# Row maxima of the first 20 steps taken over pairs of key blocks: a + relu(b - a)

## The chip, the core and the metric

The kernel runs on one core of one Trainium2 chip. The metric is the device time of one execution in microseconds (us), lower is better. TensorE is written PE (PEld is its weight load), VectorE is DVE, ScalarE is ACT, GpSimd is POOL, and SP issues the transfers.

## What is computed

One transformer block on 2048 rows of 448: layer norm, attention with 16 heads of 28 that share one key and one value head, a residual, layer norm, a SwiGLU feed-forward with 1792 hidden columns, and a residual.

```python
def _A_ref(x, wq, wk, wv, wo):
    q = (x @ wq).reshape(B, S, H, Dh).transpose(0, 2, 1, 3)
    k, v = x @ wk, x @ wv
    p = softmax(einsum("bhqd,bkd->bhqk", q, k) * Dh ** -0.5)
    o = einsum("bhqk,bkd->bhqd", p, v)
    return o.transpose(0, 2, 1, 3).reshape(B, S, H * Dh) @ wo
def _B_ref(x, w1, w3, w2):
    return (silu(x @ w1) * (x @ w3)) @ w2
h = x + _A_ref(layernorm(x), ...)
out = h + _B_ref(layernorm(h), ...)
```

## The kernel before

The 2048 rows are four tiles `t` of 512. Queries are worked on in 16 items `i = 4 t + g`, one for each tile and each group `g` of four heads; the four heads of a group lie in four lanes of 32 partitions, so four matmuls with 32 rows of weights run side by side in the array. `KH` holds the keys (high part) of all 2048 rows, copied into all four lanes, `KL` the low part, `QR[t]` the queries, `QS[i]` one item's queries, split into a high and a low part.

The softmax needs the maximum of each row of scores before the exponential. An item has 16 steps `(n, kt)`, 128 queries against 512 keys. In a step, `Unit.mm` writes four 128x512 score blocks, one a head, into four PSUM banks, and `Unit.red` reduces each with one DVE `tensor_reduce` to one column of `MX[i]`. A function `quad` does the four units of one step. After 16 steps `max_done` takes the maximum over the four columns and `max_out` writes it, by transfers, into row 28 of `QS[i]`; row 28 of each lane of `KH` holds ones, so that the later score matmul has the maximum already subtracted. In the main loop of 256 steps `Head.mm` makes those scores (three matmuls a head), ACT takes the exponential, `pv` multiplies by the values, and beside them the loop does the units that are `AHEAD = 20` steps further on. So the first 20 steps of units lie ahead of the loop. They are the list `first` of 20 quads, taken out one by one by `quads()`, between the matmuls of the start-up stage: `tr(t)` transposes the normed rows, `kv(t)` makes keys and values of tile `t` in 11 matmuls, `q(t, g)` makes queries in 11 matmuls. `kv` and `q` call `quads` after their sixth matmul (`between`).

All engines run in program order, the order of the Python calls. PSUM has seven banks for all this, handed out by `bank()` in the order in which `done()` gave them back. In `kv(t)`, ACT writes the keys into `KH[0:64]`, then SP issues three transfers one after the other: the copy to `KH[64:128]`, the ones into row 28 of each lane (which must wait for the copy, since two of its rows lie there), and the copy of `KL`.

Of the kernel before, what the change touches and what calls it, by code (L numbers as in the profile page):

```python
# [8 lines left out]
F32 = mybir.dt.float32  # L9
F32R = mybir.dt.float32r  # L10
AF = mybir.ActivationFunctionType
ALU = mybir.AluOpType
# [4 lines left out]
P = 128  # L17
# [5 lines left out]
T = 512  # L23
NT = S // T
NQ = T // P
NG = H // 4
NC = S // P
NF = F // P
NI = NT * NG
EPS = 1e-5  # L30
SCALE = DH ** -0.5
AHEAD = 20
ORDER = "3a u2 w 0a 2a u1 3b 1a 0b 2b 3c 1b 0c 2c u3 v u0 1c".split()
# [4 lines left out]
def block_kernel(  # L38
# [13 lines left out]
    ve, se, ge, pe, sy = nc.vector, nc.scalar, nc.gpsimd, nc.tensor, nc.sync  # L52
# [4 lines left out]
    def f(ap):  # L57
        return ap.bitcast(F32)
# [6 lines left out]
    wk_pool = ctx.enter_context(tc.tile_pool(name="work", bufs=2))  # L65
# [9 lines left out]
    KH = keep.tile([P, S], F32R, name="KH", tag="kh")  # L75
# [37 lines left out]
    def bank(name="pb"):  # L113
        k = free.pop(0)
        ps = ps_w.tile([P, T], F32, name=name, tag=f"bank{k}") if k < 7 else ps_o.tile([P, T], F32, name=name, tag="po")
        used[id(ps)] = ps, k
        return ps

    def done(ps):
        free.append(used.pop(id(ps))[1])  # L120
# [20 lines left out]
    def load_w(dst, w):  # L141
        sy.dma_start(dst[:, 0:3], w[0:384].rearrange("(c p) m -> p c m", p=P))
        sy.dma_start(dst[0:64, 3], w[384:448])
        sy.dma_start(dst[64:128, 3], w[384:448])
# [11 lines left out]
    def ln_stats(t, n):  # L156
        if n == 0:
            LN[t] = (ln_pool.tile([P, NQ, 6], F32, name="st"),
                     ln_pool.tile([P, NQ, 2], F32, name="mv"),
                     ln_pool.tile([P, NQ], F32, name="rs"), {}, ln_pool.tile([P, NQ], F32, name="nb"))  # L160
        st, mv, _, _, _ = LN[t]
        ve.bn_stats(st[:, n], X[t][:, n])  # L162
        ve.bn_aggr(mv[:, n], st[:, n])

    def ln_rstd(t, n0=0, n1=NQ):
        _, mv, rs, _, nb = LN[t]
        ve.tensor_scalar(rs[:, n0:n1], mv[:, n0:n1, 1], EPS, None, op0=ALU.add)
        ge.tensor_tensor(rs[:, n0:n1], rs[:, n0:n1], pexp[:, n0:n1], op=ALU.pow)
# [44 lines left out]
    QS, MX, PT, PO, WH, WS = {}, {}, {}, {}, {}, {}  # L213
# [12 lines left out]
    def lane(j):  # L226
        return slice(32 * j, 32 * j + 32)
# [17 lines left out]
            ve.tensor_reduce(MX[self.i][:, c, self.kt : self.kt + 1], self.ps, axis=AX.X, op=ALU.max)  # L245
            done(self.ps)

    def quad(i, n, kt):
        us = [Unit(i, n, kt, j) for j in range(4)]
        for u in us:  # L250
            u.mm()
        for u in us:
            u.red()

    def max_done(i):

# [11 lines left out]
    class Head:  # L268
# [14 lines left out]
        def exp(self):  # L283
            i, c, (p, jj) = self.i, self.c, divmod(self.j, 2)
            if (i, c, p) not in PT:
                PT[i, c, p] = p_pool.tile([P, 2, T], F32R, name="pt")
            se.activation(f(PT[i, c, p][:, jj]), self.ps, AF.Exp, bias=0.0, scale=SCALE)  # L287
            done(self.ps)
# [78 lines left out]
    with tc.tile_pool(name="start", bufs=1) as sp:  # L367
        wq_r = wo_r = OT[:, :, :D]
        WQ = [w.rearrange("p c (h r) -> p c h r", h=H) for w in OS]
        wkv_r = sp.tile([P, 4, 96], F32, name="wkv_r")  # L370
        WKV = [sp.tile([P, 4, 96], F32R, name=f"WKV{k}") for k in range(2)]
        ones = sp.tile([4, T], F32, name="ones")
        ve.memset(wkv_r, 0.0)
        ve.memset(ones, 1.0)
        ve.memset(VA, 1.0)
        for k in range(2):
            ve.memset(f(NEG[k]), 0.0)
        for k in range(2):
            ve.memset(f(WQ[k][:, :, :, DH:]), 0.0)
        for m0, w in ((0, wk), (64, wv)):  # L380
            load_w(wkv_r[:, :, m0 : m0 + DH], w)
        sy.dma_start(X[1], xv[1])
        load_w(wq_r, wq)
        for t in range(2, NT):
            sy.dma_start(X[t], xv[t])

        def split_wkv():
            ve.tensor_copy(wkv_r[:, :, 32 : 32 + DH], wkv_r[:, :, :DH])
            se.activation(WKV[0], wkv_r, AF.Copy)
            ge.tensor_tensor(WKV[1], wkv_r, f(WKV[0]), op=ALU.subtract)  # L390

        def split_wq():
            wq4 = wq_r.rearrange("p c (h r) -> p c h r", h=H)
            for c in range(4):
                se.activation(WQ[0][:, c, :, :DH], wq4[:, c], AF.Copy)
                eng = ge if c < 2 else ve
                eng.tensor_tensor(WQ[1][:, c, :, :DH], wq4[:, c], f(WQ[0][:, c, :, :DH]), op=ALU.subtract)

        def load_wo():
            ge.memset(wo_r, 0.0)  # L400
            wov = wo.rearrange("(g j r) e -> j r g e", j=4, r=DH)
            for j in range(4):
                sy.dma_start(wo_r[32 * j : 32 * j + DH], wov[j])

        def split_wo(g):
            ve.tensor_copy(WO[0][:, g], wo_r[:, g])
            ge.tensor_tensor(WO[1][:, g], wo_r[:, g], f(WO[0][:, g]), op=ALU.subtract)

        def stats(t, *ns):
            for n in ns:  # L410
                ln_stats(t, n)
            if NQ - 1 in ns:
                ln_rstd(t)

        def norm(t):
            for n in range(NQ):
                ln_norm(t, n)

        def tr(t, *cs):
            for c in cs or range(4):  # L420
                ln_tr(t, c)

        def kv(t, between=None):
            cols = slice(t * T, (t + 1) * T)
            ps = bank()
            mm_D(ps[:96], WKV, XT[t], slice(0, 96), slice(0, T), between)
            se.activation(KH[0:64, cols], ps[0:64], AF.Copy)
            ve.tensor_tensor(KL[0:64, cols], ps[0:64], f(KH[0:64, cols]), op=ALU.subtract)
            vt = sp.tile([P, T], F32, name="vt", bufs=2)
            se.activation(vt[64:96], ps[64:96], AF.Copy)  # L430
            sy.dma_start(f(KH[64:128, cols]), f(KH[0:64, cols]))
            sy.dma_start(f(KH[28::32, cols]), ones)
            sy.dma_start(f(KL[64:128, cols]), f(KL[0:64, cols]))
            done(ps)
            return vt

        def va(t, vt):
            ps = bank()
            for n in range(NQ):
                pe.transpose(ps[:, 32 * n : 32 * n + 32], vt[64:96, n * P : (n + 1) * P], ident[64:96, 64:96])  # L440
            ve.tensor_copy(VA[:, NQ * t : NQ * t + NQ, :DH],
                           ps[:, :P].rearrange("p (n r) -> p n r", n=NQ)[:, :, :DH])
            done(ps)

        def q(t, g, between=None):
            ps = bank()
            mm_D(ps, [w[:, :, 4 * g : 4 * g + 4].rearrange("p c h r -> p c (h r)") for w in WQ],
                 XT[t], slice(0, P), slice(0, T), between)
            if t == g == 0:
                build_qs(0, ps)  # L450
            else:
                se.activation(QR[t][:, g], ps, AF.Copy)
            done(ps)

        first = [(quad, 0, n, kt) for kt in range(4) for n in range(NQ)]
        first += [(max_done, 0), (max_out, 0)]
        first += [(quad, 1, *divmod(c, 4)) for c in range(AHEAD - NC)]

        def quads(n=1):
            while n > 0 and first:  # L460
                fn, *args = first.pop(0)
                fn(*args)
                n -= fn is quad

        for n in range(NQ):
            ln_stats(0, n)
            ln_rstd(0, n, n + 1)
            if n > 0:
                ln_norm(0, n - 1)
        ln_norm(0, NQ - 1)  # L470
        split_wkv()
        tr(0, 0, 1)
        stats(1, 0)
        tr(0, 2)
        stats(1, 1)
        tr(0, 3)
        stats(1, 2, 3)
        split_wq()
        v0 = kv(0)
        norm(1)  # L480
        q(0, 0)
        tr(1)
        stats(2, 0, 1, 2, 3)
        va(0, v0)
        q(0, 1)
        v1 = kv(1)
        norm(2)
        stats(3, 0, 1, 2, 3)
        q(0, 2)
        q(0, 3)  # L490
        build_qs(1)
        tr(2)
        va(1, v1)
        quads()
        v2 = kv(2, quads)
        norm(3)
        q(1, 0, quads)
        quads()
        q(1, 1, quads)
        va(2, v2)  # L500
        quads()
        q(1, 2, quads)
        build_qs(2)
        q(1, 3, quads)
        tr(3)
        v3 = kv(3, quads)
        load_wo()
        for t in (2, 3):
            for g in range(NG):
                if g % 2 == 0:  # L510
                    quads()
                if (t, g) == (2, 1):
                    va(3, v3)
                q(t, g, quads)
        quads(64)
# [16 lines left out]
    for i in range(NI - 1):  # L532
        e = NC * (i + 1)
# [3 lines left out]
    for t in range(NT - 1):  # L537
        e = NC * NG * (t + 1)
# [33 lines left out]
    for s in range(LAST):  # L572
        i, c = divmod(s, NC)
# [156 lines left out]
```

## Time and profile before

| what | us |
|---|---|
| median of 3 runs (lowest, highest) | 1247.76 (1244.99, 1248.25) |
| the profiled execution, its time | 1245.28 |
| the same, span of the trace | 1243.5 |
| PE, DVE, ACT, POOL busy in the span | 1214.8, 892.4, 658.0, 336.5 |
| the 80 reductions of the 20 quads, DVE busy | 48.5 |
| the start-up stage with the quads | 40 to 99.94 |
| the main loop's first matmul | 99.94 |

Times in the trace count from the start of the span. A row of the timeline has its start, its length, engine, line, operation and tiles, how many instructions it stands for, and in brackets the idle time ahead of it and what ended that. Busy PE time is modelled for pipelined matmuls, so PE's pace is read from the starts of consecutive rows.

### The profile page before, as it was taken

What the parts mean: (1) busy time and instruction counts of PE and PEld (TensorE: products, weight loads), DVE (VectorE), ACT (ScalarE), POOL (GpSimd) and SP (SyncE); (2) the same over time, 40 slices, a digit from 0 to 9 for tenths busy, and PEclk for the clock granted to TensorE, in tenths of its full rate; (3) what the DMA queues carried; (4) which work ended last, traced back from release to release, by engine and by line L of the source; (5) the groups of instructions that cost most, each with busy time, mean ns of one, the idle gap of its engine ahead of it and who ended that gap; (6) DMA issues with size and microseconds to landing.
All of it is one profiled execution on the core that took longest, in us unless ns stands there. A gap on an engine that the chain in (4) does not pass through costs nothing. (4 is left out here: it accounts for less than half of the span.)

```text
span 1243.5 us, 25301 instructions
## 1 busy us (share of the span) xinstructions
PE 1214.8 (98%) x10492; PEld 725.0 (58%) x10492; DVE 892.4 (72%) x1474; ACT 658.0 (53%) x1251; POOL 336.5 (27%) x270
## 2 busy tenths in 40 slices
PE   5999999999999999999999999999999999999998
PEld 4665444444544444444444443488888888888876
DVE  7999999999798998898998894144445445444333
ACT  3226888887698886688886688721111111121111
POOL 3201011100112110111110110454555555555552
PEclk8999999999999999999999999999999999999999
DMA  4010001000001000000000010023000000000000
GB/s 160 18 36 2 11 24 45 11 11 2 10 9 38 11 11 2 10 27 20 11 11 1 11 37 11 22 68 105 8 1 30 1 1 30 1 1 30 1 1 30
DMA packets 32411, 27.03 MB, mean 22 GB/s; under 512 B 10840, under 2 KB 28952, under 8 KB 32296
## 3 DMA queue, kind: packets, MB, share of 16 engines
q1 hardware_dynamic: 32296, 25.41, 7.0%
q8 instruction: 82, 1.34, 0.5%
q14 instruction: 33, 0.27, 0.1%
HBM read 20.25 MB, written 3.80 MB: 19 GB/s over the span
## 5 line engine op out<-in xcount | busy, mean ns | idle before, releaser
L245 DVE TENSOR_REDUCE mx<-pa 128x1 f32<-128x512 f32 x1024 | 633.7, 680 | 18.3 <-PE pa L240 6.8
L287 ACT ACTIVATE pt<-pb 128x512 f32<-128x512 f32 x1024 | 530.8, 604 | 144.5 <-PE pb L278 127.4
L278 PE MATMUL pb<-qs,KH 32*128 32x512 f32 x2048 | 368.3, 451 | 3.2 <-ACT pt L287 0.3
L240 PE MATMUL pa<-KH,qs 32*128 32x512 f32 x1024 | 362.2, 469 | 5.8 <-DVE mx L245 2.6
L295 PE MATMUL po<-pt,VA 128*32 128x256 f32 (+1 forms) x3936 | 326.7, 400 | 0.5 <-ACT OT L299 0.5
L278 PE MATMUL pb<-qs,KL 32*128 32x512 f32 x1024 | 274.9, 420 | 0.0
L278 PEld LDWEIGHTS pb<-qs,KH 32*128 32x128 f32 x2048 | 166.7, 182 | 140.4 <-ACT pt L287 89.8
L240 PEld LDWEIGHTS pa<-KH,qs 32*128 32x128 f32 x1024 | 147.3, 181 | 112.8 <-DVE mx L245 99.9
L134 PE MATMUL pa<-xh,qs 128*128 128x512 f32 x784 | 206.2, 396 | 0.0
L134 PEld LDWEIGHTS pa<-xh,qs 128*128 128x128 f32 x784 | 146.7, 188 | 34.5 <-issue 1.2
L622 ACT ACTIVATE rb<-pa 128x512 f32<-128x512 f32 x56 | 30.5, 596 | 253.1 <-PE pa L614 253.1
L295 PEld LDWEIGHTS po<-pt,VA 128*32 128x32 f32 x3936 | 79.8, 108 | 135.5 <-issue 126.8
L639 PE MATMUL pb<-w2s,pt 128*128 128x448 f32 x672 | 144.5, 370 | 0.8 <-POOL w2s L350 0.8
L639 PEld LDWEIGHTS pb<-w2s,pt 128*128 128x128 f32 x672 | 124.0, 188 | 21.0 <-issue 10.2
L278 PEld LDWEIGHTS pb<-qs,KL 32*128 32x128 f32 x1024 | 116.2, 183 | 0.8
L342 POOL TENSOR_TENSOR qs<-QR,qs 128x1024 fp32r<-128x1024 f32 x32 | 88.0, 2766 | 98.7 <-DVE qs L341 98.7
L631 DVE TENSOR_TENSOR pt<-rb,pt 128x512 fp32r<-128x512 f32 x56 | 82.4, 1471 | 39.2 <-ACT pt L630 39.2
L341 DVE CAST qs<-QR 128x1024 fp32r<-128x1024 f32 x32 | 21.0, 688 | 120.5 <-PE pa L614 96.7
L134 PE MATMUL pa<-xl,qs 128*128 128x512 f32 x336 | 96.2, 394 | 0.0
L630 ACT ACTIVATE pt<-rb 128x512 fp32r<-128x512 f32 x56 | 35.5, 633 | 81.5 <-DVE rb L627 81.5
L221 POOL TENSOR_TENSOR qs<-QR,qs 128x512 fp32r<-128x512 f32 x15 | 19.3, 1283 | 206.2 <-ACT qs L220 190.2
L134 PEld LDWEIGHTS pa<-xl,qs 128*128 128x128 f32 x336 | 63.2, 188 | 14.9
(91 smaller groups left out, 756.7 us busy)
## 6 DMA issues: line engine op xcount, KB each, us to landing
rb<-sd SPq DMA_DIRECT2D x64, 64.0 KB
QR<-in_B_w_dram SPq DMA_DIRECT2D x16, 192.0 KB
X<-in_A_x_dram SPq DMA_DIRECT2D x3, 896.0 KB
out_dram<-X SPq DMA_DIRECT2D x3, 896.0 KB
w<-in_B_w_dram SPq DMA_DIRECT2D x8, 192.0 KB
w_wo<-in_B_w_dram SPq DMA_DIRECT2D x6, 224.0 KB
qs<-ngt SPq DMA_DIRECT2D x64, 2.0 KB
sm<-OT SPq DMA_DIRECT2D x64, 2.0 KB
```

The costliest lines, as they stand in the source:

```text
L134: pe.matmul(ps, lhs[b][:, cb, lsl], rhs[a][:, ca, rsl], start=(k == 0), stop=(k == len(terms) - 1 and not part),)
L240: pe.matmul(self.ps, QS[i][r, 0, n * P : (n + 1) * P], KH[r, kt * T : (kt + 1) * T], start=True, stop=True)
L245: ve.tensor_reduce(MX[self.i][:, c, self.kt : self.kt + 1], self.ps, axis=AX.X, op=ALU.max)
L278: pe.matmul(self.ps, (KH, KH, KL)[k][r, c * P : (c + 1) * P], QS[i][r, (0, 1, 0)[k]], start=(k == 0), stop=(k == 2))
L287: se.activation(f(PT[i, c, p][:, jj]), self.ps, AF.Exp, bias=0.0, scale=SCALE)
L295: pe.matmul(PO[i][32 * j : 32 * j + 32, q], VA[:, c], f(PT[i, c, j // 2][:, j % 2, q]), start=(c == 0 and h0 == 0), stop=(c == NC - 1 and ...
L341: ve.tensor_copy(wh, W13[k])
L342: ge.tensor_tensor(wl, W13[k], f(wh), op=ALU.subtract)
L622: se.activation(sg, ps[0], AF.Silu)
L630: se.activation(h[:, 0], sg, AF.Copy)
L631: ve.tensor_tensor(h[:, 1], sg, f(h[:, 0]), op=ALU.subtract)
L639: pe.matmul(Y[t][n][:, :D], hid[a][:, n * P : (n + 1) * P], w2s[:, b, :D], start=(k == 0 and m == 0), stop=(k == NF - 1 and m == 2))
```

## The change

`quad` takes a pair of 512-key blocks `kp` instead of one. With a = q·k0 and b = q·k1, max(a, b) = a + relu(b − a). POOL makes `KD[kp]`, the difference of the keys of the two blocks, once a pair. A quad with `diff=True` multiplies the queries by `KD` into four banks, and ACT writes relu of each into a tile `rb`. The following quad with `diff=False` multiplies by the keys of the pair's first block, and one DVE instruction a head adds the bank to `rb`, writes the sum back into `rb`, and puts the maximum over its 512 columns into `MX`. Of the four columns of `MX` for a row two are written, the other two keep a very low value from a POOL memset. There are still 20 quads of four matmuls, ten of each kind; the units in the main loop stay as they were. `kv(3)` has no quad between its matmuls any more. `vt` has one buffer instead of two, and the transfer of the ones is cut into 64 pieces of 128 B instead of 4 of 2 KB.

```diff
-    def quad(i, n, kt):
-        us = [Unit(i, n, kt, j) for j in range(4)]
-        for u in us:
-            u.mm()
-        for u in us:
-            u.red()
+    RL = {}
+
+    def quad(i, n, kp, diff):
+        for j in range(4):
+            if i not in MX:
+                MX[i] = wk_pool.tile([P, 16, 4], F32, name="mx")
+                ge.memset(MX[i], LOW)
+            ps = RL[j, diff] = bank("pa")
+            ks = KD[:, kp] if diff else KH[:, 2 * kp * T : (2 * kp + 1) * T]
+            pe.matmul(ps, QS[i][lane(j), 0, n * P : (n + 1) * P], ks[lane(j)], start=True, stop=True)
+        for j in range(4):
+            ps = RL.pop((j, diff))
+            if diff:
+                r = RL[j] = (wk_pool if j % 2 else sp).tile([P, T], F32, name="rb", bufs=2)
+                se.activation(r, ps, AF.Relu)
+            else:
+                r = RL.pop(j)
+                ve.tensor_tensor_reduce(r, ps, r, 1.0, LOW, op0=ALU.add, op1=ALU.max,
+                                        accum_out=MX[i][:, 4 * j + n, 2 * kp : 2 * kp + 1])
+            done(ps)
...
-        ones = sp.tile([4, T], F32, name="ones")
+        KD = sp.tile([P, 2, T], F32R, name="KD")
+        ones = sp.tile([64, 32], F32, name="ones")
...
-            vt = sp.tile([P, T], F32, name="vt", bufs=2)
+            vt = sp.tile([P, T], F32, name="vt")
             se.activation(vt[64:96], ps[64:96], AF.Copy)
             sy.dma_start(f(KH[64:128, cols]), f(KH[0:64, cols]))
-            sy.dma_start(f(KH[28::32, cols]), ones)
+            sy.dma_start(f(KH[28::32, cols]).rearrange("j (b e) -> j b e", b=16), ones)
             sy.dma_start(f(KL[64:128, cols]), f(KL[0:64, cols]))
+            if t % 2:
+                ge.tensor_tensor(KD[:, t // 2], f(KH[:, cols]), f(KH[:, (t - 1) * T : t * T]), op=ALU.subtract)
...
-        first = [(quad, 0, n, kt) for kt in range(4) for n in range(NQ)]
+        first = [(quad, 0, n, kp, diff) for kp in range(2) for n in range(NQ) for diff in (True, False)]
         first += [(max_done, 0), (max_out, 0)]
-        first += [(quad, 1, *divmod(c, 4)) for c in range(AHEAD - NC)]
+        first += [(quad, 1, 0, kp, diff) for kp in range(2) for diff in (True, False)]
...
-        v3 = kv(3, quads)
+        v3 = kv(3)
```

On PE, from the transposes of tile 3 (L193) through the matmuls of `kv(3)` (those with `WKV`, the key and value weights) to those of `q(2, 0)` (with `OS`, where the query weights lie), before:

```order
L193 MATMUL pb<-ident,xn 128x128 x16
L134 MATMUL pb<-xh,WKV_118 96x512 x3
L134 MATMUL pb<-xl,WKV_118 96x512 x3
L240 MATMUL pa<-KH,qs 128x512 x4
L134 MATMUL pb<-xh,WKV_119 96x512 x3
L134 MATMUL pb<-xh,WKV_118 96x512
L134 MATMUL pb<-xh,WKV_119 96x512
L240 MATMUL pa<-KH,qs 128x512 x4
L134 MATMUL pb<-xh,OS_100 128x512 x3
```

The same place on PE now (lines moved by one, the quads are L258):

```order
L194 MATMUL pb<-ident,xn 128x128 x16
L135 MATMUL pb<-xh,WKV_118 96x512 x3
L135 MATMUL pb<-xl,WKV_118 96x512 x3
L135 MATMUL pb<-xh,WKV_119 96x512 x3
L135 MATMUL pb<-xh,WKV_118 96x512
L135 MATMUL pb<-xh,WKV_119 96x512
L258 MATMUL pa<-KD,qs 128x512 x4
L135 MATMUL pb<-xh,OS_100 128x512 x3
```

The quad inside `kv(3)` is gone, so eight quads instead of nine stand ahead of the end of `kv(3)`; the quad right behind it now multiplies by `KD`, whose second half is made from the keys of `kv(3)` itself.

On POOL, from the normalisation constants of tile 2 (`nb`) on, with what each instruction waits for (DMAHW stands for transfers), before:

```order
L171 TENSOR_SCALAR nb<-nb 128x4 [waits Pool_49]
L181 COPY xn<-xn 128x64 [waits DVE_49,PE_49] x4
L168 TENSOR_TENSOR rs<-rs,pexp 128x4 [waits DVE_49]
L170 TENSOR_TENSOR nb<-mv,rs 128x4 [waits Pool_49]
L171 TENSOR_SCALAR nb<-nb 128x4 [waits Pool_49]
L221 TENSOR_TENSOR qs<-QR_93,qs 128x512 [waits Activation_49]
L181 COPY xn<-xn 128x64 [waits DVE_49,PE_49] x4
L221 TENSOR_TENSOR qs<-QR_93,qs 128x512 [waits Activation_49]
L400 MEMSET OT 128x4x448 [waits DMAHW5_49,DMAHW4_49]
```

And now:

```order
L172 TENSOR_SCALAR nb<-nb 128x4 [waits Pool_49]
L451 TENSOR_TENSOR KD<-KH 128x512 [waits DMAHW3_49,DMAHW1_49,DMAHW4_49,DMAHW0_49,Activation_49]
L182 COPY xn<-xn 128x64 [waits DVE_49,PE_49] x4
L169 TENSOR_TENSOR rs<-rs,pexp 128x4 [waits DVE_49]
L171 TENSOR_TENSOR nb<-mv,rs 128x4 [waits Pool_49]
L172 TENSOR_SCALAR nb<-nb 128x4 [waits Pool_49]
L222 TENSOR_TENSOR qs<-QR_93,qs 128x512 [waits Activation_49]
L255 MEMSET mx 128x64
L182 COPY xn<-xn 128x64 [waits DVE_49,PE_49] x4
L222 TENSOR_TENSOR qs<-QR_93,qs 128x512 [waits Activation_49]
L451 TENSOR_TENSOR KD<-KH 128x512 [waits DMAHW6_49,DMAHW2_49,DMAHW7_49,DMAHW1_49,Activation_49]
L416 MEMSET OT 128x4x448 [waits DMAHW5_49]
```

The first difference of keys stands ahead of the copies that complete the normed rows of tile 2 (`xn`), the second ahead of the memset of `OT`; both wait for the copy and the ones of two `kv` calls.

On DVE, the first quads before (four reductions a quad, then the low keys of `kv(2)`, the normed rows of tile 3 and on), and now:

```order
L245 TENSOR_REDUCE mx<-pa 128x1 x8
L428 TENSOR_TENSOR KL<-pb,KH 64x512
L179 TENSOR_SCALAR xn<-X_83,mv,rs 128x448 x4
L245 TENSOR_REDUCE mx<-pa 128x1 x12
L441 COPY VA<-pb 128x4x28
```

```order
L266 ISA rb,mx<-pa,rb 128x512
L266 ISA mx 128x1
L266 ISA rb,mx<-pa,rb 128x512
L266 ISA mx 128x1
L266 ISA rb,mx<-pa,rb 128x512
L266 ISA mx 128x1
L266 ISA rb,mx<-pa,rb 128x512
L266 ISA mx 128x1
L444 TENSOR_TENSOR KL<-pb,KH 64x512
L180 TENSOR_SCALAR xn<-X_83,mv,rs 128x448 x4
```

Each sum with its maximum is two instructions on DVE, the second one column wide, and a pair of quads has four of them where it had eight reductions.

More of the change, by code (lines that the diff above doesn't have):

```diff
@@ L30 @@
 EPS = 1e-5
+LOW = -3.0e38
 SCALE = DH ** -0.5
```

## The prediction

> **What bounds the kernel now.** I first read the busy times by stage, cut at the start of the quads (40), the end of `kv(3)` on PE (69.14), and the first and last matmuls of the main loop (99.94, 757).
>
> ```profile
> core 0: us, PE busy (x) PEld busy (x) DVE busy (x) ACT busy (x) POOL busy (x), PEclk, DMA share, GB/s
> 40.00:69.14 29.14, 26.91 (x127) 16.23 (x126) 28.40 (x50) 7.44 (x14) 6.66 (x10) 1.00 0.04 10
> 69.14:99.94 30.80, 30.20 (x138) 19.34 (x137) 29.01 (x51) 5.37 (x9) 0.20 (x1) 1.00 0.16 36
> 99.94:757.00 657.06, 650.43 (x7708) 297.58 (x7707) 605.97 (x1029) 515.15 (x997) 84.97 (x98) 1.00 0.06 15
> ```
>
> The change touches only the first two rows. DVE is busy 57.41 of their 59.94 us, ACT 12.81, POOL 6.86. PE looks nearly as busy, but its matmul ends are modelled, so I ask the groups of 40 to 99.9 and the waits of 38 to 100 which of the two holds the other.
>
> ```profile
> L245 DVE TENSOR_REDUCE mx<-pa 128x1 f32<-128x512 f32 x80 | 48.5, 676 | 1.3 <-PE pa L240 1.2
> PEld pa L240 <- DVE mx L245: 6.0, 13, 1.5
> ```
>
> The 80 reductions waited 1.3 us in all, while PE's quads alone waited 6.0 us for them: the stage goes at DVE's pace. How much it can shrink is PE's own pace, from its weight loads.
>
> ```profile
> 82.50 0.64 PEld L134 LDWEIGHTS pb<-xl,OS 128*128 128x128 f32 x3
> 83.49 0.19 PEld L240 LDWEIGHTS pa<-KH,qs 32*128 32x128 f32 x4 [0.35 <-DVE mx L245]
> 83.92 0.99 PEld L134 LDWEIGHTS pb<-xh,OS 128*128 128x128 f32 x5 [0.24 <-issue]
> 88.17 1.69 PEld L134 LDWEIGHTS pb<-xh,OS 128*128 128x128 f32 x8 [0.24 <-issue]
> 89.90 0.64 PEld L134 LDWEIGHTS pb<-xl,OS 128*128 128x128 f32 x3
> 63.49 1.91 PEld L193 LDWEIGHTS pb<-ident,xn 128*128 128x128 f32 x16
> 67.39 0.19 PEld L240 LDWEIGHTS pa<-KH,qs 32*128 32x128 f32 x4 [0.25 <-issue]
> 74.14 0.32 PEld L440 LDWEIGHTS pb<-ident,vt 32*128 32x128 f32 x4 [0.37 <-DVE mx L245]
> ```
>
> Eight matmuls from 88.17 to 89.90 are 0.216 us each, so a `q` of 11 is 2.38. From 82.50 to 83.92 lie three such (0.65) and a quad: a quad costs 0.77, say 0.78. Transposes and six matmuls of `kv(3)` with their waits for DVE and ACT take 67.39 − 0.25 − 63.49 = 3.65, its last five 1.08; a `va` takes 0.32 + 0.37 = 0.69.
>
> **The change, step by step.**
>
> *DVE and ACT lose the bound.* The prices:
>
> ```profile
> 76.62 12.27 DVE L245 TENSOR_REDUCE mx<-pa 128x1 f32<-128x512 f32 x20 [0.55 <-PE pa L240]
> 39.96 1.89 DVE L207 TENSOR_TENSOR xl<-pb,xh 128x512 fp32r<-128x512 f32 x3 [0.51 <-ACT xh L200]
> 30.67 0.18 DVE L163 BATCH_NORM_AGGREGATE mv<-st 128x2 f32<-128x6 f32 x1
> 30.77 0.59 DVE L162 BATCH_NORM_STATS2 st<-X 128x6 f32<-128x448 f32 x1
> 39.34 2.05 ACT L200 ACTIVATE xh<-pb 128x512 fp32r<-128x512 f32 x4
> L631 DVE TENSOR_TENSOR pt<-rb,pt 128x512 fp32r<-128x512 f32 x56 | 82.4, 1471 | 39.2 <-ACT pt L630 39.2
> ```
>
> A reduction takes 12.27/20 = 0.61. No row shows the new instruction. Nearest is a sum of a bank and an SBUF tile of the same size (L207), 0.63; the one-column read behind it I take like the small instruction at 30.67, which holds the next one up 0.10. So 0.73 for one, 40 × 0.73 = 29 us for 80 × 0.61 = 49. The upper end is the two-tile sum of L631, 1.47; but both its operands are in SBUF and it runs where POOL is half busy, while POOL is nearly idle here, so L207 stands nearer. ACT gains 40 relus at 2.05/4 = 0.51, 20.5 us on top of 12.81, in 59.94. A pair of quads then costs DVE 2.9 and ACT 2.1, and PE 2 × 0.78 + 1.2 `q` = 4.4. PE becomes the bound. Seven banks hold a quad, a `q` and half the next quad; the third and fourth bank of a quad wait for the first two DVE sums of the one before, done about 2.0 us after it began, just when PE comes. I put 0.5 us of such waits on each half of the stage (0 to 2).
>
> *First part, 40 to 45.56: 0.* `KD[0]` needs the ones of `kv(1)` and stands ahead of the copies that the last four transposes of tile 2 need.
>
> ```profile
> 41.90 0.48 PEld L134 LDWEIGHTS pb<-xh,WKV 128*96 128x96 f32 x3 [0.42 <-DVE xl L207]
> 45.56 0.42 PEld L134 LDWEIGHTS pb<-xh,OS 128*128 128x128 f32 x2
> 36.20 0.55 SPq L432 DMA_DIRECT2D KH<-ones  x1
> 323.24 0.35 SPq L312 DMA_DIRECT2D sd<-sm  x1
> 324.73 1.70 SPq L315 DMA_DIRECT2D rb<-sd  x4
> 69.87 0.46 SPq L431 DMA_DIRECT2D KH<-KH  x1
> 72.09 0.55 SPq L432 DMA_DIRECT2D KH<-ones  x1
> 61.96 1.29 POOL L221 TENSOR_TENSOR qs<-QR,qs 128x512 fp32r<-128x512 f32 x1 [11.45 <-ACT qs L220]
> 35.16 1.59 POOL L181 COPY xn<-xn 128x64 f32<-128x64 f32 x4 [0.68 <-DVE xn L179]
> ```
>
> How long the ones take in 64 pieces no row shows: an 8 KB transfer frees its follower after 1.49 (323.24 to 324.73), the key copy after 2.22 (69.87 to 72.09). So the ones have landed at 37.7 to 38.4, `KD` (a POOL subtraction of this size, 1.29) is done at 39.0 to 39.7, the copies (1.59) at 40.6 to 41.3, against 36.75 before, and the last transposes come 0.7 to 1.4 late; but PE stood waiting for DVE to free banks until 41.90 anyway, where `kv(2)` began, and `q(1, 0)` at 45.56. Between −0.35 and +0.35 remains; I take 0. The memset of `mx` comes right behind on POOL, ahead of the first sum. The transfer issue itself moves past nothing on SP.
>
> *45.56 to the end of `kv(3)`: −3.4.* Before 69.14 − 45.56 = 23.58. Now four `q` (9.5), six quads instead of seven (4.7), one `va` (0.7), transposes and `kv(3)` (4.7): 19.6, with 0.5 of waits 20.1, and 0.1 for rounding. DVE has 12 sums there, 8.8 us.
>
> *The second difference: +6.1.* The quad behind `kv(3)` needs `KD[1]`, hence the keys of `kv(3)` themselves, and PE's whole queue stands behind it.
>
> ```profile
> 69.14 0.29 PEld L240 LDWEIGHTS pa<-KH,qs 32*128 32x128 f32 x4 [0.39 <-issue]
> 69.25 0.59 ACT L427 ACTIVATE KH<-pb 64x512 fp32r<-64x512 f32 x1 [2.78 <-PE pb L134]
> ```
>
> On the clock of before: PE is ready at 69.14, ACT has the keys at 69.84, their copy goes at 69.87, the ones at 72.09 and land at 73.6 to 74.3, `KD[1]` is done at 74.9 to 75.6. PE stands 5.7 to 6.5 us, 6.1. Nothing covers it: 12 quads and eight `q` are queued behind, and DVE and ACT have only leftovers. The `wo` transfers behind the `OT` memset start some 4 us later than before and are wanted in the loop's second step.
>
> *PE comes back at half clock: +2.1.* The trace has one such stop.
>
> ```profile
> 21.65 0.80 PE L134 MATMUL pb<-xh,OS 128*128 128x512 f32 x1 [4.39 <-POOL OS L397]
> 20.00:22.00 2.00, 0.35 (x1) 0.50 0.31 70
> 26.00:28.00 2.00, 2.00 (x16) 0.80 0.00 0
> 22.74 2.07 PE L134 MATMUL pb<-xh,OS 128*128 128x512 f32 x4 [0.29 <-POOL OS L397]
> 29.63 1.09 PE L134 MATMUL pb<-xh,OS 128*128 128x512 f32 x4
> 24.61 2.99 PE L193 MATMUL pb<-ident,xn 128*128 128x128 f32 x16
> 38.12 1.91 PE L193 MATMUL pb<-ident,xn 128*128 128x128 f32 x16
> ```
>
> After 4.39 us of standstill the granted clock was 0.50 until about 26.8 (0.80 is the mean of that window), and the same work took 2.07 for 1.09 and 2.99 for 1.91: 2.06 lost. A stop of 6.1 should do the same; ends: 0, and half of the 5.15 us from 21.65 to 26.8, 2.6.
>
> The Trainium skill, TensorE: Matmul & The Clock Gate, Part 1, says that the clock falls to half after an idle window of about 3.4 us and is back after about 3.4 us of sustained work. This trace agrees with the fall (idle 4.39, clock 0.50), but shows 5.15 us of slow work, not 3.4; by the page's figure the term would be an estimated 1.7, and the sum 0.4 less. It is a rule that speaks against this change.
>
> *69.14 to 99.94 without the stop: −1.2.* Before 30.80 with 11 quads; now eight `q` (19.0), `va` (0.7), 12 quads (9.4), 29.1, with 0.5 of waits 29.6.
>
> *Into the loop: +0.8.*
>
> ```profile
> 89.59 9.61 DVE L245 TENSOR_REDUCE mx<-pa 128x1 f32<-128x512 f32 x16
> 100.50 5.00 DVE L245 TENSOR_REDUCE mx<-pa 128x1 f32<-128x512 f32 x8 [1.30 <-PE pa L240]
> ```
>
> Before, the quads were used up three half-`q`s ahead of the loop, and DVE stood idle 1.30. Now the last quad stands inside the last `q`, 2.1 us ahead of the loop; its four sums end 3.5 after its start, where the loop's first reduction could start at 2.7. In the loop DVE is busy 92%, so little of it is made up (0 to 1.5). The maximum of item 0 is still out some 12 us of PE work ahead of the loop, against about 8 it needs.
>
> Sum: 0 − 3.4 + 6.1 + 2.1 − 1.2 + 0.8 = **+4.4 us**. The profiled execution (1245.28, of which 1243.5 is span) would become 1249.7; it lies 2.5 under the median of the runs, 1247.76, on which I put the forecast: 1252.2, say **1252**. With all ends the same way: −0.4 − 3.9 + 5.7 + 0 − 1.7 + 0 = −0.3, and +0.4 − 2.0 + 6.5 + 2.6 + 0.3 + 1.5 = +9.3.
>
> **Rivals.**
>
> *The stop is hidden, and the kernel is faster.* If `KD[1]` were ready when PE comes, 6.1 and 2.1 go and the sum is −3.8: 1244.0. For it: every other part of the stage gains. Against it: the order has no matmul between `kv(3)` and the quad, and three steps in a row follow those matmuls. It decides only from a stop under about 4 us.
>
> *PE's pauses around quads go too.* Of a quad's 0.78, 0.35 ahead of its loads is pause. If that were DVE's doing, 18 quads give 6.3 more, sum −1.9: 1245.9. The 0.35 at 83.49 is put down to DVE; but the same pause stands in the profile as issue time elsewhere, and PE's 0.24 behind the quad as well.
>
> *The new DVE instruction is slow.* From 1.1 us each (four of them as long as PE's 4.4) DVE is the bound again. At L631's 1.47 + 0.10 the 24 sums of the second half need 38 us for 29.6, the 12 of the first 19 us beside 5.5 of other work, so 24 for 20: +4.4 + 8 + 4 = 16, 1264.
>
> *Bank waits at their end or a longer stop*: +9, 1257.
>
> **How the numbers follow.** A measurement tells about 0.3%, 3.7 us, from nothing. My case has 0.72; 4.4 lies just past the bound, and its spread (−0.3 to +9.3) puts 0.43 of it slower and 0.29 within. Hidden stop 0.05, faster. Pauses gone 0.08: 0.05 within, 0.03 faster (if the clock holds as well). Slow instruction 0.07 and long waits 0.08, slower. So faster 0.08, same 0.34, slower 0.58. The range goes from the low end of my case, 1247, to its high end, 1257; it leaves out the hidden stop, the slow instruction and most of the vanished pauses.
>
> **What would show it.** PE idle about 6 us right behind `kv(3)`, released by POOL `KD`, with granted clock 0.5 in the microseconds behind it; `kv(3)` ending some 3.4 us earlier than 69.14; DVE busy about 20 us less in the stage; the loop's first matmul near 104 instead of 99.94, and the loop as long as before. I am wrong if PE has work during the wait for `KD[1]`, if the clock stays at 1.00, or if a sum with maximum takes well over 0.73.

## The result and the profile after

The changed kernel takes 1249.04 us in the median of 15 runs (1247.57 to 1253.08), the kernel before 1246.51 in 15 runs beside them (1244.71 to 1248.25): a ratio of 1.0024, with a 95% interval of 1.0014 to 1.0034. It is slower by 2.5 us in the medians and 3.0 by the ratio, less than the 0.3% that the prediction took as the least that a measurement can tell, but the interval lies wholly above 1. The forecast was 1252, in a range of 1247 to 1257. The profiled execution took 1248.07, with a span of 1246.3, 2.8 more than the 1243.5 before.

First the busy times by stage (PEclk is the granted clock, the share of full speed that PE was given), cut at the first matmul of `q(1, 0)` (45.56 before), where the quad behind `kv(3)` would have been loaded (64.50, worked out below), where it was (70.81), and at the loop's first matmul.

```profile
core 0: us, PE busy (x) PEld busy (x) DVE busy (x) ACT busy (x) POOL busy (x), PEclk, DMA share, GB/s
40.00:44.30 4.30, 4.09 (x22) 2.27 (x22) 2.96 (x8) 2.73 (x6) 2.28 (x5) 1.00 0.00 0
44.30:64.50 20.20, 20.14 (x101) 13.03 (x99) 14.33 (x40) 11.92 (x23) 2.89 (x5) 1.00 0.07 15
64.50:70.81 6.31, 0.10 (x1) 0.00 (x1) 0.68 (x1) 1.18 (x2) 1.32 (x2) 0.67 0.20 43
70.81:102.36 31.55, 31.43 (x140) 19.89 (x141) 14.45 (x46) 16.05 (x31) 1.76 (x3) 0.90 0.12 26
102.36:806.40 704.04, 696.72 (x8132) 315.18 (x8132) 613.77 (x1043) 557.47 (x1080) 95.97 (x106) 1.00 0.06 15
```

DVE's busy time between 40 and the loop fell from 57.41 to 32.42 us. The second row lasts 20.20 where it was 23.58. Then PE does almost nothing for 6.31 us, and the fourth row runs at a mean clock of 0.90. The last row ends with the loop's last copy, and here is the same stretch of the kernel before:

```profile
99.94:803.20 703.26, 695.82 (x8132) 314.42 (x8132) 611.89 (x1037) 557.39 (x1080) 96.00 (x106) 1.00 0.06 15
```

Both hold 8132 matmuls; the loop took 0.78 us longer. (The 757 at which the prediction cut the loop is ahead of its last item; the loop ends at these later times.)

The stop itself, in the timeline from the end of `kv(3)` on:

```profile
63.03 1.10 PEld L135 LDWEIGHTS pb<-xh,WKV 128*96 128x96 f32 x5
64.63 0.59 ACT L443 ACTIVATE KH<-pb 64x512 fp32r<-64x512 f32 x1 [2.25 <-PE pb L135]
65.25 0.46 SPq L447 DMA_DIRECT2D KH<-KH  x1
67.47 0.57 SPq L448 DMA_DIRECT2D KH<-ones  x1
69.49 1.26 POOL L451 TENSOR_TENSOR KD<-KH 128x512 fp32r<-128x512 f32 x1 [9.76 <-issue]
70.81 0.29 PEld L258 LDWEIGHTS pa<-KD,qs 32*128 32x128 f32 x4 [6.68 <-POOL KD L451]
```

The last weights of `kv(3)` are in at 64.13; with the pause of 0.39 that a quad had there before, its loads would start at 64.5. Keys at 65.22, their copy 2.22 from issue to follower, the ones 2.02 until POOL starts, 1.26 of subtraction: each step follows the one ahead, and nothing of PE lies between. The waits of 38 to 105 (who waited for whom: us in all, times, longest) name the same, and that PE no longer waits much for DVE:

```profile
PEld pa L258 <- POOL KD L451: 6.7, 1, 6.7
DVE rb L266 <- PE pa L258: 26.0, 8, 9.4
PEld pb L135 <- DVE mx L266: 0.4, 1, 0.4
```

The granted clock, in windows of PE alone, and the same five matmuls of a `q` slow and fast:

```profile
66.00:68.00 2.00, 0.00 (x0) 0.65 0.30 66
68.00:70.00 2.00, 0.00 (x0) 0.50 0.32 70
74.00:76.00 2.00, 2.00 (x8) 0.50 0.92 220
76.00:78.00 2.00, 2.00 (x10) 0.79 0.60 114
...
75.13 1.77 PEld L135 LDWEIGHTS pb<-xh,OS 128*128 128x128 f32 x5 [0.44 <-issue]
79.64 1.00 PEld L135 LDWEIGHTS pb<-xh,OS 128*128 128x128 f32 x5 [0.24 <-issue]
```

The clock fell at 66.6 (0.65 is full clock for 0.6 of the two us and half for the rest), some 2 us after PE's last work, and came back near 76.8 (0.79 is a mean of 0.5 and 1.00): six microseconds of slow work behind the stop.

And the instruction that no row of before had, on DVE:

```profile
43.54 0.69 DVE L266 CUSTOM_DVE_ANT_0 rb<-pa,rb 128x512 f32<-128x512 f32 x1 [1.27 <-PE pa L258]
44.15 0.08 DVE L266 DVE_READ_ACCUMULATOR2_ANT mx<- 128x1 f32 x1
44.15 0.69 DVE L266 CUSTOM_DVE_ANT_0 rb<-pa,rb 128x512 f32<-128x512 f32 x1
...
L266 DVE CUSTOM_DVE_ANT_0 rb<-pa,rb 128x512 f32<-128x512 f32 x40 | 25.2, 687 | 26.1 <-PE pa L258 26.0
```

The next one starts 0.61 us behind the last, and the read of the maximum lies inside that time: adding two blocks with a maximum costs DVE what one plain reduction of the same size did. DVE idles 26 us for PE ahead of these sums.

### The profile page after: what moved, and what is told of

Read it like the earlier page. It is cut to its first block, busy times and chain, and to the rows that moved or that the text cites. A ratio compares the mean times of both kernels' runs of the same rounds, so it can differ in the third digit from the quotient of the medians.

```text
span 1246.3 us, 25411 instructions
## 1 busy us (share of the span) xinstructions
PE 1214.9 (97%) x10492; PEld 725.7 (58%) x10492; DVE 869.0 (70%) x1474; ACT 677.7 (54%) x1291; POOL 337.9 (27%) x274
## 5 line engine op out<-in xcount | busy, mean ns | idle before, releaser
L246 DVE TENSOR_REDUCE mx<-pa 128x1 f32<-128x512 f32 x944 | 585.8, 682 | 15.4 <-PE pa L241 5.5
L241 PE MATMUL pa<-KH,qs 32*128 32x512 f32 x944 | 347.4, 467 | 3.6 <-DVE mx L246 1.2
L241 PEld LDWEIGHTS pa<-KH,qs 32*128 32x128 f32 x944 | 141.2, 181 | 101.8 <-DVE mx L246 93.2
```

The costliest lines, as they stand in the source:

```text
L241: pe.matmul(self.ps, QS[i][r, 0, n * P : (n + 1) * P], KH[r, kt * T : (kt + 1) * T], start=True, stop=True)
```

## The experiments

Theory: the stage was at DVE's pace, and the change makes it shorter by some 4.6 us (−3.4 and −1.2), but the wait for `KD[1]`, the clock that falls in it, and the late sums at the loop's start cost 9. Rivals: the new instructions or their bank waits keep the stage long without the wait, or the clock's fall costs nothing. All profiles below are one execution each. The following table collects, for each kernel, the time from the first matmul of `q(1, 0)` to the loop's first, and the ratio to before; the start of `q(1, 0)` lay between 44.06 and 45.60 in the ten kernels that have the changed order up to there, so it is taken out.

| kernel | `q(1, 0)` to loop, us | median, us | ratio to before, 95% interval |
|---|---|---|---|
| before | 54.38 | 1246.51 | 1 |
| after | 58.06 | 1249.04 | 1.0024 (1.0014 to 1.0034) |
| no wait (1) | 50.28 | 1242.36 | 0.9968 (0.9956 to 0.9980) |
| stop filled (2) | 55.34 | 1248.53 | 1.0019 (1.0009 to 1.0028) |
| half reductions (3) | 48.37 | 1239.95 | 0.9951 (0.9939 to 0.9964) |
| two `q` ahead (4) | 51.34 | 1242.66 | 0.9972 (0.9963 to 0.9981) |
| `KD` ahead of the ones (5) | 54.94 | 1246.37 | 0.9998 (0.9990 to 1.0007) |
| both, one `q` (6) | 53.22 | 1243.22 | 0.9973 (0.9963 to 0.9983) |
| both, two `q` (7) | 50.64 | 1244.20 | 0.9981 (0.9972 to 0.9991) |
| first pair only (8) | 50.24 | 1241.88 | 0.9960 (0.9949 to 0.9972) |
| the same, quad in `kv(3)` (9) | 51.42 | 1241.10 | 0.9955 (0.9940 to 0.9969) |
| no wait, quad in `kv(3)` (10) | 50.57 | 1240.53 | 0.9949 (0.9936 to 0.9961) |

**1. The wait taken away.** Both pairs multiply by the first difference:

```diff
-            ks = KD[:, kp] if diff else KH[:, 2 * kp * T : (2 * kp + 1) * T]
+            ks = KD[:, 0] if diff else KH[:, 2 * kp * T : (2 * kp + 1) * T]
```

> The changed kernel, but the quads of the second pair multiply by the first pair's key difference (left out: the second pair's own difference, so the subtracted maxima are other numbers). All instructions and their number stay, only TensorE's wait for the second difference goes. Theory (the stop behind kv(3) costs its 6.3 us and another 2.9 us at half clock, and nothing downstream takes any of it back): 9 us under the changed kernel, about 1240, some 6 us under the kernel before, clock 1.00 from 62 us on, first matmul of the loop near 93. Rival (the stop is absorbed, the 2.5 us are the price of the new operations): within 1 us of the changed kernel, 1248 to 1250.

Measured 1242.36 (1239.92 to 1244.62), ratio 0.9968. The loop starts at 94.98, 7.4 earlier than in the changed kernel, and the clock is 1.00 from 64 to 96. So the wait with what follows from it is what makes the change a loss. That it ended 2 us above the expectation has a place in the trace that no theory named, the loop's first microseconds:

```profile
92.00:96.00 4.00, 3.92 (x21) 1.00 0.00 0
96.00:100.00 4.00, 3.79 (x26) 0.78 0.00 0
100.00:104.00 4.00, 4.00 (x34) 0.50 0.00 0
104.00:108.00 4.00, 4.00 (x52) 0.87 0.02 4
```

PE is busy there, but the clock falls to half. What that cost is worked out below, under *Into the loop*.

**2. The stop filled.** 26 matmuls that feed nothing stand between `kv(3)` and the quad, so that PE is not idle while it waits:

```diff
         v3 = kv(3)
+        fill = ps_o.tile([P, T], F32, name="po")
+        for _ in range(26):
+            pe.matmul(fill, WQ[0][:, 0, 0:4].rearrange("p h r -> p (h r)"), XT[3][0][:, 0], start=True, stop=True)
```

> The changed kernel with 26 matmuls of 128x512 (5.6 us at 0.216 each) put on TensorE behind kv(3), into a bank that nobody reads: the stop keeps its length, but TensorE works in it. Theory (half clock behind the stop costs about 2.9 us, in some executions more): 3 us under the changed kernel, about 1246, granted clock 1.00 from 60 to 80 us, and the times lie within 2 us of each other where the changed kernel's lie 5.5 apart. Rival (the clock costs nothing, since DVE or ACT would hold the stage anyway): 1249, same spread.

```profile
64.85 5.88 PEld L527 LDWEIGHTS po<-xh,OS 128*128 128x128 f32 x26
71.41 0.19 PEld L258 LDWEIGHTS pa<-KD,qs 32*128 32x128 f32 x4 [0.68 <-POOL KD L451]
...
71.41:100.32 28.91, 28.79 (x141) 1.00 0.13 29
```

The clock stayed at 1.00, and the stretch from the quad to the loop took 28.91 instead of 31.55: the fallen clock costs 2.64 us. The ten runs lie within 1.8 us of each other (clock 0.996 or 0.997), those of the changed kernel within 5.5 (0.990 to 0.996, the slowest at 0.990). But the time, 1248.53, did not follow: it is the rival's 1249, while clock and spread are the theory's. The maxima's transposes, one an item, tell where the gain went in the profiled execution. In this kernel:

```profile
174.94 0.21 DVE L275 STREAM_TRANSPOSE ngt<-neg 128x32 f32<-128x32 f32 x1 [0.30 <-POOL neg L274]
216.91 0.21 DVE L275 STREAM_TRANSPOSE ngt<-neg 128x32 f32<-128x32 f32 x1 [0.30 <-POOL neg L274]
```

and in the changed kernel:

```profile
176.20 0.21 DVE L275 STREAM_TRANSPOSE ngt<-neg 128x32 f32<-128x32 f32 x1 [0.30 <-POOL neg L274]
217.16 0.21 DVE L275 STREAM_TRANSPOSE ngt<-neg 128x32 f32<-128x32 f32 x1 [0.30 <-POOL neg L274]
```

This item takes 41.97 us here and 40.96 there. The four items from 133 us on take 41.73 to 42.31 here and 40.91 to 41.16 there, 4.0 us more in all; two later items bring 1.4 back, and the whole loop is 2.5 us longer, as much as the clock had gained. So the loop can run at a second, slower gait for some items; what chose it here stays open, and the price of the clock is shown in the stage alone.

**3. Is DVE the bound before?** The kernel before, its 80 reductions of the quads over half their columns:

```diff
-            u.red()
+            u.red(T // 2)
```

> The kernel before, but the 80 reductions of the first 20 quads read 256 columns instead of 512 (left out: half the scores in those maxima). It does the relief of DVE alone: no new wait, no work on ACT or GpSimd. Theory (DVE's reductions set the pace of 40 to 99.9, TensorE could go 5 to 6 us faster): about 1241, first matmul of the loop near 94.5. Rival (TensorE sets the pace itself, the waits for DVE are only where its own slack shows): 1246 to 1247.

Measured 1239.95 (1239.01 to 1241.11), ratio 0.9951; the loop starts at 93.66 instead of 99.94. Four reductions now take 1.42 us instead of 2.45, and DVE waits for PE ahead of them:

```profile
64.55 1.42 DVE L245 TENSOR_REDUCE mx<-pa 128x1 f32<-128x256 f32 x4 [0.26 <-PE pa L240]
```

So the stage goes at PE's pace, as the prediction's first part has it.

**4. Work put into the wait.** The changed kernel, with `q(2, 0)`, `va(3)` and `q(2, 1)` ahead of the quad that needs `KD[1]`:

```diff
-                if g % 2 == 0:
+                late = (t, g) in ((2, 0), (2, 1))
+                if not late:
                     quads()
...
-                q(t, g, quads)
+                q(t, g, None if late else quads)
```

> The changed kernel with q(2,0), va(3) and q(2,1) moved ahead of the first quad of the second pair, and the remaining 12 quads spread over the other six q. Theory (the stop is an order on TensorE's queue that 5.4 us of other work can fill): stop about 1 us instead of 6.3, clock 1.00, 8 us under the changed kernel, about 1241, so 5 under the kernel before. Rivals: the denser quads at the end wait for DVE's sums (2.45 us a pair against 3.9 of TensorE, so it should not): 1243 to 1246; or the stop only moves: 1249.

```profile
71.43 0.19 PEld L258 LDWEIGHTS pa<-KD,qs 32*128 32x128 f32 x4 [0.99 <-POOL KD L451]
```

Of 6.7 us 0.99 is left, the loop starts at 96.28 with the clock at 1.00 from 40 us on, and the time is 1242.66, ratio 0.9972, between the theory's 1241 and the first rival's 1243. In this order the change is a gain of some 3.5 us; the place of the quads that need `KD[1]` had turned it into a loss.

**5. A shorter chain.** `KD` stands ahead of the transfer of the ones, so it waits for the key copy alone (the ones then overwrite row 28 of the keys, not of `KD`):

```diff
-            sy.dma_start(f(KH[28::32, cols]).rearrange("j (b e) -> j b e", b=16), ones)
-            sy.dma_start(f(KL[64:128, cols]), f(KL[0:64, cols]))
             if t % 2:
                 ge.tensor_tensor(KD[:, t // 2], f(KH[:, cols]), f(KH[:, (t - 1) * T : t * T]), op=ALU.subtract)
+            sy.dma_start(f(KH[28::32, cols]).rearrange("j (b e) -> j b e", b=16), ones)
+            sy.dma_start(f(KL[64:128, cols]), f(KL[0:64, cols]))
```

> The changed kernel with GpSimd's key difference issued ahead of the transfer of the ones (row 28 of the queries is zero in these quads, so the difference needs no ones). It takes one link, 2.0 us, out of the three behind kv(3). Theory (the stop is the chain ACT, key copy, ones, GpSimd, and nothing hides it): stop 4.3 instead of 6.3 us, half clock behind it as behind the 4.4 us stop of the start-up: 2 us under the changed kernel, about 1247. If a stop of 4.3 lets the clock stand, 5 under, 1244. Rival (the ones are not in the chain): 1249.

```profile
68.61 0.19 PEld L258 LDWEIGHTS pa<-KD,qs 32*128 32x128 f32 x4 [4.73 <-POOL KD L449]
...
64.00:72.00 8.00, 3.74 (x16) 0.84 0.24 60
72.00:80.00 8.00, 8.00 (x42) 0.94 0.36 74
```

The wait is 1.95 shorter, what the ones took. The clock still falls, but only near 69.5, when PE is back at work, and for 3.4 us (0.84 and 0.94 are means over 8 us). It took 1246.37, near the theory's 1247 and the same as before within the interval (0.9990 to 1.0007).

**6 and 7. Both together.** Edit 5 with `q(2, 0)` ahead of the quad and no quad in the last `q` (6), and edit 5 with edit 4 (7).

> e5 with q(2,0) ahead of the first quad of the second pair; the 12 quads are spread over seven q, and the last q has none. Theory: stop 1.9 us, clock 1.00 behind it, and no quad just ahead of the loop: 7 to 8 us under the changed kernel, about 1241. If the clock falls after a stop of 1.9: 1244. Rival (what is gained ahead of the loop, the loop gives back, in item times of 42 us instead of 40.9): 1243 to 1246.

> e5 with q(2,0), va(3) and q(2,1) ahead of the first quad of the second pair (as in e4). Theory: no stop is left (4.3 us of chain under 5.4 us of work), 1 us under e4, about 1241.5. Rival (the loop's pace decides): anywhere from 1241 to 1245, with item times to show it.

Kernel 6 keeps a wait of 2.16 us, and its clock falls at 71.0, 1.7 us after PE is back at work:

```profile
69.26 0.19 PEld L258 LDWEIGHTS pa<-KD,qs 32*128 32x128 f32 x4 [2.16 <-POOL KD L449]
...
70.00:72.00 2.00, 2.00 (x10) 0.74 0.44 89
72.00:74.00 2.00, 2.00 (x7) 0.50 0.86 206
74.00:76.00 2.00, 2.00 (x10) 0.90 0.80 175
```

It took 1243.22, between the 1241 of the theory and the 1244 that was expected if the clock fell. Kernel 7 has no wait for `KD` at all, and its loop starts at 96.17, yet it took 1244.20, between 1241.28 at clock 0.997 and 1246.34 at 0.992. Here the expectation missed by 2.7 us: in the profiled execution the clock was 1.00 from 40 us up to the loop and 0.79 in its first 8 us. The slow items of the rival do not show; the four items that were slow in kernel 2 take 40.9 here.

**8 and 9. Only what needs no wait.** Difference and relu for the first pair alone; blocks 2 and 3 by a plain reduction a head (`old`, the quad of before). In 9 also the last piece of the edit, a quad inside `kv(3)` again, which does not need `kv(3)`:

```diff
-        first = [(quad, 0, n, kp, diff) for kp in range(2) for n in range(NQ) for diff in (True, False)]
+        first = [(quad, 0, n, 0, diff) for n in range(NQ) for diff in (True, False)]
+        first += [(old, 0, n, kt) for kt in (2, 3) for n in range(NQ)]
...
-        first += [(quad, 1, 0, kp, diff) for kp in range(2) for diff in (True, False)]
+        first += [(quad, 1, 0, 0, diff) for diff in (True, False)]
+        first += [(old, 1, 0, kt) for kt in (2, 3)]
...
-        v3 = kv(3)
+        v3 = kv(3, quads)
```

> One part alone: the eight quads ahead of kv(3) and two of item 1 work on the first pair by difference and relu, the blocks 2 and 3 are reduced one by one on DVE as before (12 quads with the old reduction behind kv(3) or with them the two of item 1). No stop, since nothing waits for kv(3)'s difference. Theory (the relief of the first half is worth 3 to 4 us, the second half is then at DVE's old pace, 40 reductions and 8 sums, 29.5 us against 29 of TensorE): loop from about 96, 1242 to 1243.5. Rival (relief in one half is lost in the other, since DVE has the same work ahead of the loop): 1246.

> The pairs of blocks 0 and 1 by difference and relu, blocks 2 and 3 by one reduction a head as before, and a quad inside kv(3) as before, so that nine quads stand ahead of the end of kv(3) and the last q has none. Theory A (the quads' DVE time and the standstill are all there is to it; what the position of the last quad costs is the late start of the loop's sums and the granted clock at the loop's start): no standstill, loop from about 95.5, clock 1.00 from 40 to 120, runs close together, 1240 to 1241. Theory B (the clock's fall at the loop's start comes in some executions whatever stands in the last q): as with the last quad in the last q, 1240 to 1243, median about 1241.9, with a granted clock under 1.00 in 96 to 108 in some.

8 took 1241.88 (ratio 0.9960), 9 took 1241.10 (1240.08 to 1242.76, ratio 0.9955). Both beat the kernel before and the changed one; their intervals overlap. The six runs of 9 lie 2.7 us apart, not as close as its theory A has it. The loop's first 8 us:

```profile
96.00:104.00 8.00, 7.80 (x62) 0.79 0.00 0
```

in 8, and in 9

```profile
96.00:104.00 8.00, 7.84 (x83) 1.00 0.00 0
```

**10. No wait, and the last `q` without a quad.** Edits 1 and `kv(3, quads)`:

> The changed kernel with the second pair's first quads multiplied by the first difference (so the maxima of blocks 2 and 3 are not those of the reference), hence with no wait for the second difference, and a quad inside kv(3) again, so that the last q has none. Theory A (the clock's fall at the loop's start in the kernel without the wait came from the last quad's place): clock 1.00 from 40 to 120, loop from about 94.8, about 1240, runs within 1.5 us of each other. Theory B (it comes whatever stands in the last q): 1239.9 to 1244.6, median 1242.4, as without the quad in kv(3).

1240.53, within 1239.38 to 1241.26, clock 1.00 in the loop's first microseconds. Without the quad in `kv(3)` (1) the runs reached from 1239.92 to 1244.62. The intervals of the two ratios overlap, so theory A is favoured and not shown; and in kernel 4 the last `q` has a quad and the profiled clock stayed at 1.00. Of the profiled executions, the clock fell at the loop's start in three (1, 7, 8) of the seven whose last `q` has a quad, and in none of the five others.

A second condition sorts all twelve. The clock changed only at the steps of a grid of 3.41 us (worked out below, under *Half clock*). In kernels 1, 7 and 8 a step of it lay from 0.14 us ahead of the loop's first matmul to 0.69 behind it, and the clock fell at the next step. In the four others with a quad in the last `q` the nearest steps lay 1.05 to 2.20 us ahead and 1.21 to 2.37 behind. In kernels 6 and 10 a step lay 0.35 and 0.59 behind, but there is no such quad. This was sorted afterwards, from one execution of each kernel, and no run tested it; what makes the clock fall stays open.

## Why the prediction was right, point by point

*The bound.* Right: half-length reductions alone took 6.3 us out of the stage (3), and with DVE at 32 us the stage went at PE's pace. The waits were weak evidence for it, though: 12 of the 13 behind the 6.0 us lasted 0.29 to 0.42, about as long as the pause ahead of a quad that stayed.

*The new DVE instruction, 0.73.* It took 0.61 from start to start; the read of the maximum, put at 0.10, costs nothing. As PE was the bound this changed little, and the rival of a slow instruction falls.

*First part, 0.* `q(1, 0)` began at 44.30 instead of 45.56, −1.26, outside the −0.35 to +0.35 that the prediction left. Part of that is luck: the slow clock of the start-up, back at 26.8 in the trace of before, was back at 25.6 here:

```profile
22.00:24.00 2.00, 1.41 (x4) 0.56 0.01 2
24.00:26.00 2.00, 2.00 (x11) 0.59 0.00 0
```

The ten kernels with this order began `q(1, 0)` at 44.06 with the clock back at 25.1, at 44.69 to 44.98 with the clock back at 26.6 to 27.1, and at 45.51 to 45.60 with it back at 28.1 to 28.6. So an estimated 0.4 to 0.7 of the 1.26 is the clock's, and 0.6 to 0.9 is the change's, which the prediction put at nothing. How much of that is DVE's relief was not separated.

*45.56 to the end of `kv(3)`, −3.4.* 20.20 for 23.58: −3.4.

*The second difference, +6.1.* 6.3. The transfer in 64 pieces, which no row of before showed, took 2.02 (1.5 to 2.2 were the bounds).

*Half clock, +2.1.* Against the filled stop 2.64, above the upper end of 2.6 by a hair; the term copied 2.06 from a single earlier stop, as if one stop were like another. Read in windows of 0.1 us, the slow stretches of all twelve executions (ahead of the program's last microseconds) last 3.41, 6.83 or 10.24 us: the one here 10.24 (66.60 to 76.84), those of the start-up 6.83 (19.98 to 26.81 in the kernel before) or 3.41 (22.23 to 25.64 in the changed one). Falls in one execution lie whole multiples of 3.413 apart, in the changed kernel 22.23 and 66.60 (13 of them), in kernel 1 19.74 and 98.25 (23). So the clock changed only on a grid of 3.41 us, which lies otherwise in each execution; how much slow work stands behind a stop, 5.15 us then and 6.0 now, depends on where the stop falls in that grid as well as on its length. That the term came so near is in part luck.

The Trainium skill (TensorE: Matmul & The Clock Gate, Part 1) gives about 3.4 us of sustained work until the clock is back; here it was 6.0. The same section calls the ramp run-variable, and that agrees: runs of the changed kernel differ by 5.5 us with the mean clock, those with the stop filled by 1.8. It gives an idle window of about 3.4 us for the fall; kernel 6 shows a fall around a stop of 2.16, and in the changed kernel the clock fell some 2 us into the stop.

*69.14 to 99.94, −1.2.* 31.55 less 2.64 is 28.91, −1.9: the bank waits, put at 0.5, were hardly there, since DVE came out of the stop with nothing to do. Without the stop (1) the same stretch took 30.08, so the forecast of 29.6 was about right for a DVE that is still behind.

*Into the loop, +0.8.* The loop took 704.04 instead of 703.26, +0.78, and all of it lies ahead of the loop's second transpose of maxima (the first one stands ahead of the loop), before and now:

```profile
132.05 0.21 DVE L260 STREAM_TRANSPOSE ngt<-neg 128x32 f32<-128x32 f32 x1 [0.30 <-POOL neg L259]
135.26 0.21 DVE L275 STREAM_TRANSPOSE ngt<-neg 128x32 f32<-128x32 f32 x1 [0.30 <-POOL neg L274]
```

From the loop's first matmul that is 32.11 us before and 32.90 now. It was 32.07 to 32.11 in the five kernels whose last `q` has no quad (before, 3, 6, 9, 10) and 32.89 to 32.91 in the four that have one and kept the clock there (after, 2, 4, 5): the term and its cause are right. In 1, 7 and 8 it was 35.39, 34.1 and 33.97, so the clock's fall at the loop's start cost 2.5, 1.2 and 1.1 us there.

Stage and loop together are 3.68 + 0.78 = +4.5, where the sum had +4.4. That they agree so well is luck: +0.2 for the stop and +0.5 for the clock were missed one way and −0.7 for the stretch behind it the other. The span grew by 2.8 because the start of `q(1, 0)` came 1.26 earlier and the part behind the loop took 0.4 less, neither of which the sum had; the medians differ by 2.5. The forecast of 1252 lies 3 us above 1249.04 for this, and because it stood on 1247.76, a median of three runs, where 15 gave 1246.51. On the rivals: the stop was not hidden. PE's pauses around quads stayed (0.35 to 0.37 ahead of the loads, put down to issue). The sum with the stop hidden, −3.8, is what kernels 1 and 4 then showed: ratios of 0.9968 and 0.9972 are −4.0 and −3.5 us.

## What to carry to other kernels

When a change takes work off the bounding engine by deriving an operand from freshly made data, follow the whole chain of that operand (eviction, each transfer, the derivation) to the engine whose queue stands behind it: here 3.4 + 1.9 us of gain met 6.3 us of standstill and 2.6 of cold clock. Look for independent work already in the program to put ahead of the waiting instruction, or apply the change only to the part whose operands are early; the second pair's quads moved behind two `q`, or one pair instead of two, made a loss of 0.2% a gain of 0.3 to 0.45%. A stop on PE is to be priced at its length plus half of the slow work behind it, as a range and not as one number: the slow stretch lasted one, two or three steps of 3.41 us, and the runs scatter with it (5.5 us, against 1.8 with the stop filled).

## What had not been expected of the hardware

- A DVE sum of a PSUM bank and an SBUF tile of 128x512 with a maximum over its columns, and the read of the accumulator, follow each other in 0.61 us, as plain reductions of one bank do.
- The granted clock changed only on a grid of 3.41 us: slow stretches of 3.41, 6.83 and 10.24 us, and falls in one execution 13 to 23 whole steps apart.
- It fell around a standstill of only 2.16 us (kernel 6), and at the loop's start with no standstill at all (kernels 1, 7, 8: 0.50 for 6.8, 3.4 and 3.4 us), where matmuls with 32 rows of weights wait in short pauses for DVE and ACT.
- The main loop, the same program in all kernels, has two gaits: four items took 40.9 to 41.2 us in eleven profiled executions and 41.7 to 42.3 in that of kernel 2; the clock was 1.00 in both.
